# Groups of ten pairs in place of groups of four, six and eight, and another way for the down results, in a transformer block on one core

## The chip, the cores and the metric

One core of one Trainium2 chip runs the whole block. The metric is the device time of one execution in microseconds (us).

## The reference

The input is x, 2048 rows of 512, in f32. A vector c, through silu and a matrix, gives six modulation vectors (sa, ca, ga, sb, cb, gb). The block is

```python
h = _layernorm(x, axis=-1) * (1 + ca) + sa
x = x + ga * _A_ref(h, A_wqkv, A_wo)
h = _layernorm(x, axis=-1) * (1 + cb) + sb
x = x + gb * _B_ref(h, B_w_gate, B_w_up, B_w_down)
```

`_A_ref` is softmax attention with 32 heads of 16 columns over all 2048 rows, with an output projection wo. `_B_ref` is (silu(h @ w_gate) * (h @ w_up)) @ w_down with 1792 inner columns. All is f32, and the kernel keeps the accuracy by splitting operands into a high and a low part and adding three products.

## The kernel before

**Stages.** A projection stage (about the first tenth) makes q, k and v. Then comes attention, with the output projection and the feed-forward part of earlier rows woven into it, and at the end a tail with what is left of the third chunk and all of the fourth.

**Attention.** The 2048 query rows are four chunks of 512 (`NC`). A unit is one chunk with a group of four heads: `NU` = 32 units, eight to a chunk. A unit has 16 steps, one to each 128 keys, and a step has four pairs (`pair_of`). A pair is two matmuls of 512 columns that use different halves of TensorE's rows and run side by side: a score (line 507) and a maximum (line 478). The score goes through ScalarE's exp (line 509) into a tile `pt_` in SBUF. The maximum belongs to a unit 22 steps ahead: VectorE reduces its bank to one number for each row (line 480), which that unit's exps subtract later. For the last 22 steps no maximum is left. The product of exps and v comes later, by halves: a pv half (`pv_step`, line 522) is four heads by 256 columns, each in two passes, accumulated in bank 7. A step gives two halves. After a unit's last half ScalarE copies bank 7 to `o` (line 526), and the next unit's first half needs the bank empty.

**Order.** The order is written out by hand, as the Python code records it, and each engine works through its own list in that order. `plain(steps)` records windows of three pairs (`WIN`), after each of which some pv halves stand (`HALVES`). `filled(places, work)` records one group: after pair r it takes `places[r]` fills from `work`. A fill is two matmuls over 64 rows each (line 730), for two output banks side by side; the banks are 3 and 6 (`FBANKS`). Then it runs the callbacks in `posts` (`hook`) and those in `tails` (`flush`), and ends with pv halves (`pvs`). In a group the scores and maxima take five banks in turn (`five`: 0, 1, 2, 4, 5), a score and then its pair's maximum; behind the last maximum `ALONE` gives other places and banks for scores alone.

**What is woven in.** For each of the first three chunks: two output-projection tiles (`out_pair`, 24 fills each), a plain stretch of `NORM` and `WIN` steps for the layer norm, then the jobs of the feed-forward part: 14 gate/up tiles of 24 fills (`gate_up`) and 14 down tiles of 12 (`down`). The third chunk keeps its last seven jobs (`KEEP`) for the tail. The function `window` chooses the places. Early jobs are thin: `SIX`, six pairs and six fills to a group, four groups to a gate/up tile and two to a down tile. Later ones, from `THICK`, are thick: `TWO`, eight pairs and 12 fills, two groups to a gate/up tile, and `FOUR`, four pairs and six fills, two to a down tile. Projection tiles use `TWO`. The first down tile of the last pair of inner tiles has the places `LATE` where it is thin.

**Results of the tiles.** When a gate/up tile's fills end, ScalarE makes a tanh (`th`, line 783); at the group's end VectorE makes `q` and `m32` (lines 787 and 789) and GpSimd splits that into `mid`. When a down tile's fills end, VectorE adds both banks to the chunk's rows `x2` (line 803), at once, ahead of the reduces of the pairs that still follow in the group. After a chunk's last down tiles GpSimd's queue stores the rows (line 805) and loads those of the next chunk into the same `x2` (`rows_of`, line 642).

**Exp tiles.** `PTS` = 13 tiles `pt_` go round as a ring; a step's four tiles come free after its second pv half.

Of the kernel before, what the change touches and what calls it, by code (L numbers as in the profile page):

```python
# [9 lines left out]
F32 = mybir.dt.float32  # L10
# [9 lines left out]
P = 128  # L20
# [8 lines left out]
CW = S // NC  # L29
NG = H // 4  # L30
NU = NG * NC
NF = F // P
FG = 2
# [6 lines left out]
WIN = 3  # L40
HALVES = (2, 1, 1, 2)
ORDER = (0, 2, 1, 3)
UG = 16 * NG
PTS = 13
FBANKS = (3, 6)
KEEP = 7
NORM = 9
STARTS = (144, 272, 400)
REST = 12
THICK = (8, 8, 5)  # L50
TWO = (0, 3, 2, 2, 2, 2, 1, 0)
SIX = (0, 2, 2, 1, 1, 0)
FOUR = (0, 3, 3, 0)
LATE = (0, 0, 0, 3, 3, 0)
LAST = ((0, 4, 0, 4, 0, 4, 0, 0), (4, 5, 0, 1, 5, 0, 4, 1))
ALONE = {TWO: LAST, FOUR: ((0, 6, 0, 0), (4, 5, 0, 5)), SIX: ((0, 3, 0, 3, 0, 0), (4, 5, 0, 1, 4, 5))}


def run(it):
# [4 lines left out]
def take(it, k):  # L64
    run(islice(it, k))
# [40 lines left out]
def block_kernel(ctx, tc, x, wqkv, wo, w_gate, w_up, w_down, c, w_mod, out):  # L106
    nc = tc.nc
# [18 lines left out]
    four, bank, single = Turn(0, 1, 2, 3), Turn(4, 5, 6), Turn(7)  # L126
# [326 lines left out]
    pb = ctx.enter_context(tc.tile_pool(name="pb", bufs=2, reuse_waits="tile"))  # L453
    kop[1] = [pb.tile([P, 2, CW], F32R, name=f"kop1{c}", bufs=1) for c in range(NC)]
    pf = None
# [3 lines left out]
    qop, mx, pts, pv, o_, due, res = {}, {}, {}, {}, {}, {}, {}  # L459
    posts, tails = [], []  # L460
    n = 16 * NU
# [39 lines left out]
    def score(i, h):  # L501
        u, kt = divmod(i, 16)
        rows = slice(64 * (h % 2), 64 * (h % 2) + KR + 2)
        p_ = pb.tile([P, CW], F32, name="pt_", tag="pt", bufs=PTS)
        pts.setdefault(i, {})[h] = p_
        sp = bank("st_")
        nc.tensor.matmul(sp, kop[u % 2][kt // 4][rows, h // 2, kt % 4 * P:(kt % 4 + 1) * P], qop[u][rows, h // 2, :],  # L507
                         start=True, stop=True)
        nc.scalar.activation(p_, sp, AF.Exp, scale=SCALE)

    def pv_step(i, half):

        u, kt = divmod(i, 16)
        g = u % NG
        cols = slice(half * HQ, (half + 1) * HQ)
        if kt == 0 and half == 0:
            pv[u] = single("pv")
            o_[u] = pf.tile([P, CW], F32, name="o", tag="o", bufs=2)
        p_ = pts.pop(i) if half else pts[i]
        for h in range(4):  # L520
            e0 = (kt * H + 4 * g + h) * (DH + 1)
            nc.tensor.matmul(pv[u][32 * h:32 * h + 32, cols], v_flat[:, e0:e0 + 32], p_[h][:, cols],  # L522
                             start=(kt == 0 and half == 0), stop=(kt == 15),
                             skip_group_check=half == 1)
        if kt == 15 and half:
            nc.scalar.copy(o_[u], pv[u])  # L526
# [194 lines left out]
    def accumulate(outs, lhs, rhs, nk, after, halves, by_k=False):  # L721

        terms = [(k, a, b) for k in range(nk) for a, b in ((0, 0), (0, 1), (1, 0))]
        z = len(terms) - 1
        if halves:
            for ph in range(2):
                for j, (k, a, b) in enumerate(terms):
                    for e in range(2):
                        rows = slice(64 * (ph ^ e), 64 * (ph ^ e) + 64)
                        nc.tensor.matmul(outs[e], lhs(e, a, k)[rows], rhs(b, k)[rows],  # L730
                                         start=(ph == 0 and j == 0), stop=(ph == 1 and j == z))
                    if ph == 1 and j == z:
                        after()
                    yield
        else:
            order = [(e, j) for e in range(2) for j in range(z + 1)]
            for e, j in sorted(order, key=lambda o: o[1] // 3) if by_k else order:
                k, a, b = terms[j]
                nc.tensor.matmul(outs[e], lhs(e, a, k), rhs(b, k), start=(j == 0), stop=(j == z))  # L739
                if e == 1 and j == z:  # L740
                    after()
                yield
# [56 lines left out]
    def down(ch, m, t0, outs, halves):  # L799
        def later():  # L800
            for e in range(2):
                t = t0 + e
                nc.vector.tensor_add(ch.x2[:, t, :], outs[e], ch.x2[:, t, :])  # L803
                if m == NF // FG - 1:
                    (nc.sync if ch.ci == last else nc.gpsimd).dma_start(od[:, 4 * ch.ci + t, :], ch.x2[:, t, :])

        def after():
            if halves:
                later()
            else:  # L810
                posts.append(later)
            if t0:
                ch.load_wd(m + 1)

        mids, wd = [ch.mid[FG * m + k] for k in range(FG)], ch.wd[m]
        return accumulate(outs, lambda e, a, k: mids[k][:, a, (t0 + e) * P:(t0 + e + 1) * P],
                          lambda b, k: wd[:, b, k, :], FG, after, halves, m == NF // FG - 1)
# [20 lines left out]
    def hook():  # L838
        while posts:
            posts.pop(0)()  # L840

    def flush():
        while tails:
            tails.pop(0)()
# [66 lines left out]
    halves = [(i, half) for i in range(n) for half in range(2)]  # L911
    done, ended, owed = 0, 0, 0
# [13 lines left out]
    def pvs(most, by_halves):  # L926

        nonlocal owed
        if by_halves:
            most, owed = most + owed, 0  # L930
        while most and halves and 4 * halves[0][0] + (6 if done % 4 == 2 and not by_halves else 8) <= done:
            i, half = halves.pop(0)
            pv_step(i, half)
            most -= 1
            if i % 16 == 15 and half:
                close_unit(i // 16, done // 4 - 1)
                if by_halves:
                    break
        if by_halves and most and halves and 4 * halves[0][0] + 8 <= done:
            owed = most  # L940

    def end_steps():
        nonlocal ended
        while ended < done // 4:
            after(ended - 1)
            ended += 1

    def plain(steps, ends=()):

        nonlocal four, bank  # L950
        assert steps % WIN == 0 and done % 4 == 0
        four, bank = Turn(0, 1, 2, 3), Turn(4, 5, 6)
        for w in range(4 * steps // WIN):
            for _ in range(WIN):
                pair_of()
            if w >= 4 * steps // WIN - len(ends):
                ends[w - 4 * steps // WIN](four())
            flush()
            pvs((HALVES[(w - 2) % 4] if done > 8 else 0) + (w == 4 * steps // WIN - 1), True)
            end_steps()  # L960

    def filled(places, work):

        nonlocal four, bank
        four = bank = five
        if done >= 4 * n - 4 * (LEAD - 1):
            places, order = ALONE.get(places, (places, (4, 5, 0, 1)))
            bank = Turn(*order)
        for r in range(len(places)):
            pair_of()  # L970
            take(work, places[r])
            end_steps()
        hook()
        flush()
        pvs(3 if done % 4 else 6, False)

    def window(ch, job, args):
        thick = (args[0] if job is gate_up else 2 * args[0]) >= THICK[ch.ci]
        if job is down:
            if args == (NF // FG - 1, 0):  # L980
                return (FOUR, FOUR) if thick else (LATE, SIX)
            return (FOUR if thick else SIX,) * 2
        return (TWO,) * 2 if thick else (SIX,) * 4

    for k in range(NK):
        at(16 * (NU - 2) + 4 * k + 3, lambda k=k: chunks[last].load_wo_part(k))
    outs = [banks[b] for b in FBANKS]
    for ci in range(last):
        plain(STARTS[ci] - done // 4)
        ch = chunks[ci]  # L990
        for t0 in (0, 2):
            work = out_pair(ch, t0, outs, True)
            filled(TWO, work)
            filled(TWO, work)
        side.append(lambda: scaled(ch))
        plain(NORM)
        plain(WIN, [lambda tp, k=k: ch.turned(tp, k) for k in range(NK)])
        if ci == last - 1:
            plain(REST)
        for _ in range(len(ch.jobs) - (KEEP if ci == last - 1 else 0)):  # L1000
            job, args = ch.jobs.pop(0)
            if args == (NF // FG - 1, 0):
                chunks[ci + 1].load_wo()
            places = window(ch, job, args)
            work = job(ch, *args, outs, True)
            for group in places:
                filled(group, work)
        if ci < last - 1:
            rows_of(chunks[ci + 1])
    chunks[last - 1].load_gu(NF - 2)  # L1010

    assert done == 4 * n
    turns = chain([2, 3, 2, 0, 1, 2, 0], cycle([1, 3, 2, 0]))

# [11 lines left out]
    ch, chp = chunks[last], chunks[last - 1]  # L1026
# [56 lines left out]
```

## Time and profile before

| what | us |
|---|---|
| median of 3 runs (lowest to highest) | 1939.23 (1938.14 to 1940.55) |
| the profiled execution, its own time | 1938.7 |
| its span, first to last instruction | 1936.7 |
| TensorE busy | 1886.4 |
| VectorE busy | 1533.1 |
| ScalarE busy | 1235.0 |
| GpSimd busy | 386.5 |
| mean granted TensorE clock | 0.996 of full speed |

In the profile's rows PE is TensorE, DVE is VectorE, ACT is ScalarE and POOL is GpSimd. A row of the timeline has the start and the length in us, the engine, the line of the kernel, the operation, what it writes and reads, and how often; in brackets how long the engine was idle before it, and what ended that. In a grouped row the figures behind the bar are the busy time in us and the mean length of one in ns, and behind the next bar the idle time ahead of them. Matmuls overlap, and their ends are modelled, so their starts are what to read.

### The profile page before, as it was taken

To read this page: it belongs to the slowest core of one execution; us is meant where nothing else is said; L and a number is where in the kernel's file an instruction comes from. 1 tells how busy PE (TensorE), PEld (TensorE's weight loads), DVE (VectorE), ACT (ScalarE), POOL (GpSimd) and SP (SyncE) were. 2 spreads that over 40 slices of the span, in tenths; PEclk is the share of its full clock that TensorE was granted. 3 is DMA by queue.
4 is the path that set the end of the run, shared out by engine and by line. 5 is a ranking of instruction groups with operands and counts; after the bars stand their busy time and mean duration, and the time that the engine had idled before them with its cause. 6 is when DMAs were issued, how large, how long until landed. Compare 5 with 4: busy or idle time off the path is not lost.

```text
span 1936.7 us, 42054 instructions
## 1 busy us (share of the span) xinstructions
PE 1886.4 (97%) x16932; PEld 1231.0 (64%) x16932; DVE 1533.1 (79%) x2561; ACT 1235.0 (64%) x2330; POOL 386.5 (20%) x447
## 2 busy tenths in 40 slices
PE   7999999999999999999999999999999999997999
PEld 5766444444465666677765666677764666765887
DVE  5459999999988888888888888888889888811643
ACT  4221888888868666666667666666668666672211
POOL 3000544564213101011122101011122101120200
PEclk9999999999999999999999999999999999999999
DMA  8763655666424233334334233333433333334553
GB/s 285 276 216 120 202 174 170 199 188 202 138 75 124 75 105 124 97 116 131 110 112 136 69 110 116 113 118 111 128 106 108 92 98 116 108 134 147 180 189 109
DMA packets 102330, 267.63 MB, mean 138 GB/s; under 512 B 20552, under 2 KB 25672, under 8 KB 88952
## 3 DMA queue, kind: packets, MB, share of 16 engines
q1 hardware_dynamic: 86984, 202.27, 32.9%
q0 software_dynamic: 14464, 61.88, 9.0%
q8 instruction: 133, 2.18, 0.5%
q10 hardware_dynamic: 688, 0.80, 0.1%
q14 instruction: 61, 0.50, 0.1%
HBM read 201.85 MB, written 62.13 MB: 136 GB/s over the span
## 4 chain that ended last, share of the span: by engine, by line
PE 87%; DVE 7%; DMA 3%; ACT 2%; POOL 1%; issue 1%; SPq 0%; ACTq 0%; DVEq 0%; POOLq 0%
PE bank L522 23%; PE bank L507 19%; PE bank L730 18%; PE bank L478 11%; PE bank L739 7%; PE bank L213 7%; DVE mx L480 6%; DMA rb<-d_dr 1%; PE bank L491 1%; ACT o L526 1%; DMA dn<-o 0%; DMA d_dr<-dn 0%; PE bank L166 0%; PE bank L715 0%; DMA wm_ab<-in_w_mod 0%
## 5 line engine op out<-in xcount | busy, mean ns | idle before, releaser
L480 DVE TENSOR_REDUCE mx<-bank 128x1 f32<-128x512 f32 x2048 | 1277.9, 685 | 173.1 <-PE bank L478 133.5
L478 PE MATMUL bank<-kop,qop 48*128 48x512 f32 x2048 | 777.3, 445 | 2.3 <-DMA qop<-qd 1.5
L507 PE MATMUL bank<-qop,kop 50*128 50x512 f32 x2048 | 745.1, 422 | 3.3 <-DVE mx L480 1.2
L507 PEld LDWEIGHTS bank<-qop,kop 50*128 50x128 f32 x2048 | 347.1, 185 | 247.0 <-issue 44.1
L478 PEld LDWEIGHTS bank<-kop,qop 48*128 48x128 f32 x2048 | 343.5, 184 | 68.9 <-DVE mx L480 14.4
L730 PE MATMUL bank<-act,wgu 64*128 64x512 f32 x1872 | 356.1, 396 | 0.7 <-DVE m L789 0.6
L730 PEld LDWEIGHTS bank<-act,wgu 64*128 64x128 f32 x1872 | 236.5, 186 | 24.9 <-DVE m L789 4.2
L730 PE MATMUL bank<-wd,mid 64*128 64x512 f32 x912 | 168.8, 397 | 0.5 <-DVE m L789 0.4
L791 POOL CAST mid<-m 128x512 fp32r<-128x512 f32 x40 | 24.3, 608 | 537.3 <-DVE m L789 483.3
L730 PEld LDWEIGHTS bank<-wd,mid 64*128 64x128 f32 x912 | 112.8, 186 | 14.3 <-DVE m L789 3.2
L549 POOL TENSOR_TENSOR on<-o,rb 128x512 f32<-128x512 f32 x31 | 39.7, 1281 | 370.4 <-DMA rb<-d_dr 307.3
L213 PE MATMUL bank<-hT,wqs 128*128 128x512 f32 x384 | 96.1, 400 | 2.0 <-DVE prt L373 0.8
L787 DVE SCALAR_TENSOR_TENSOR q<-th,bank 128x512 f32<-128x512 f32 x56 | 38.0, 678 | 65.2 <-ACT th L783 65.2
L213 PEld LDWEIGHTS bank<-hT,wqs 128*128 128x128 f32 x384 | 70.2, 188 | 24.3 <-issue 6.0
L783 ACT ACTIVATE th<-bank 128x512 f32<-128x512 f32 x56 | 33.2, 594 | 58.8 <-PE bank L739 58.8
L803 DVE TENSOR_TENSOR x<-bank,x 128x512 f32<-128x512 f32 x84 | 53.7, 683 | 20.4 <-PE bank L507 20.4
L373 DVE TENSOR_TENSOR prt<-bank,prt 128x512 fp32r<-128x512 f32 x32 | 22.0, 689 | 46.7 <-ACT prt L371 44.6
L739 PE MATMUL bank<-act,kop 128*128 128x512 f32 x240 | 57.2, 396 | 0.0
L371 ACT CAST prt<-bank 128x512 fp32r<-128x512 f32 x32 | 18.8, 586 | 59.0 <-PE bank L213 50.6
L789 DVE TENSOR_TENSOR m<-bank,q 128x512 f32<-128x512 f32 x56 | 38.7, 692 | 22.0 <-PE bank L739 19.9
L739 PE MATMUL bank<-wd,mid 128*128 128x512 f32 x216 | 52.2, 395 | 0.3 <-DVE mid L792 0.3
L792 POOL TENSOR_TENSOR mid<-m,mid 128x512 fp32r<-128x512 f32 x40 | 51.5, 1288 | 3.3
(6272 smaller groups left out, 5132.9 us busy)
## 6 DMA issues: line engine op xcount, KB each, us to landing
kop<-kd SPq DMA_DIRECT2D x256, 192.0 KB
wgu<-gu_dr SPq DMA_DIRECT2D x46, 1024.0 KB
wd<-wd_dr SPq DMA_DIRECT2D x28, 1024.0 KB
gu_dr<-wgu POOLq DMA_DIRECT2D x14, 1024.0 KB, 6.7
qop<-qd SPq DMA_DIRECT2D x64, 192.0 KB
kop<-gu_dr SPq DMA_DIRECT2D x20, 512.0 KB
kd<-prt SPq DMA_DIRECT2D x16, 512.0 KB
qd<-prt SPq DMA_DIRECT2D x16, 512.0 KB
```

What stands on the lines that cost most here:

```text
L213: nc.tensor.matmul(pt, lhs(a, k), rhs(b, k), start=(n == 0), stop=(n == 3 * nk - 1))
L478: nc.tensor.matmul(pm, qop[u][rows, s, qt * P:(qt + 1) * P], kop[u % 2][kc][rows, s, :], start=True, stop=True)
L480: nc.vector.tensor_reduce(mx[u][:, b, s, qt, kc:kc + 1], pm, op=ALU.max, axis=AX.X)
L507: nc.tensor.matmul(sp, kop[u % 2][kt // 4][rows, h // 2, kt % 4 * P:(kt % 4 + 1) * P], qop[u][rows, h // 2, :], start=True, stop=True)
L522: nc.tensor.matmul(pv[u][32 * h:32 * h + 32, cols], v_flat[:, e0:e0 + 32], p_[h][:, cols], start=(kt == 0 and half == 0), stop=(kt == 15), ...
L549: mul.tensor_mul(on, o, rb)
L730: nc.tensor.matmul(outs[e], lhs(e, a, k)[rows], rhs(b, k)[rows], start=(ph == 0 and j == 0), stop=(ph == 1 and j == z))
L739: nc.tensor.matmul(outs[e], lhs(e, a, k), rhs(b, k), start=(j == 0), stop=(j == z))
L787: nc.vector.scalar_tensor_tensor(q, th, 1.0, outs[0], op0=ALU.add, op1=ALU.mult)
L789: nc.vector.tensor_mul(m32, outs[1], q)
L792: (nc.gpsimd if slow else nc.vector).tensor_sub(mid[:, 1, :], m32, mid[:, 0, :].bitcast(F32))
L803: nc.vector.tensor_add(ch.x2[:, t, :], outs[e], ch.x2[:, t, :])
```

## The change

- Groups: one shape, `TEN` (ten pairs, 12 fills), serves projection and gate/up tiles, two groups each; `FIVE` (five pairs, six fills) serves down tiles, two groups each; `LATE` is now a shape of five pairs. `window`, `THICK`, `TWO`, `SIX` and `FOUR` go. A chunk's woven work now takes 127 steps of 128, and the step left over is a plain stretch of its own.
- pv: a group ends with all halves of steps whose last score lies two pairs or more back, up to eight: six and four in turn after groups of ten; two, four, two, two after groups of five. A plain stretch ends with such a run as well, and may have a last window of fewer than three pairs. `REST` is 9 steps, not 12.
- Exp tiles: the ring is 15 long; 13 tiles lie where they lay, two (`FAR`) in the pool `pf`.
- Down results: in the groups ScalarE copies each bank to a temporary `part` and GpSimd adds that to `x2`. Both are recorded at the group's end. In the tail VectorE adds as before.

```diff
-PTS = 13
+PTS = 15
+FAR = 2
...
-REST = 12
-THICK = (8, 8, 5)
-TWO = (0, 3, 2, 2, 2, 2, 1, 0)
-SIX = (0, 2, 2, 1, 1, 0)
-FOUR = (0, 3, 3, 0)
-LATE = (0, 0, 0, 3, 3, 0)
...
+REST = 9
+TEN = (0, 2, 1, 2, 1, 2, 1, 3, 0, 0)
+FIVE = (0, 3, 1, 2, 0)
+LATE = (0, 0, 3, 3, 0)
+ALONE = {TEN: ((0, 4, 0, 4, 0, 4, 0, 0, 0, 0), (4, 5, 0, 1, 4, 5, 0, 1, 4, 5)),
+         FIVE: ((0, 3, 0, 3, 0), (4, 5, 0, 1, 5))}
...
-        p_ = pb.tile([P, CW], F32, name="pt_", tag="pt", bufs=PTS)
+        near = (4 * i + len(pts.get(i, ()))) % PTS < PTS - FAR
+        p_ = (pb if near else pf).tile([P, CW], F32, name="pt_", tag="pt", bufs=PTS - FAR if near else FAR)
...
-                nc.vector.tensor_add(ch.x2[:, t, :], outs[e], ch.x2[:, t, :])
+                if halves:
+                    part = pf.tile([P, CW], F32, name="part", tag="tmp", bufs=4)
+                    nc.scalar.copy(part, outs[e])
+                    nc.gpsimd.tensor_add(ch.x2[:, t, :], part, ch.x2[:, t, :])
+                else:
+                    nc.vector.tensor_add(ch.x2[:, t, :], outs[e], ch.x2[:, t, :])
...
-            if halves:
-                later()
-            else:
-                posts.append(later)
+            posts.append(later)
...
-        while most and halves and 4 * halves[0][0] + (6 if done % 4 == 2 and not by_halves else 8) <= done:
+        while most and halves and 4 * halves[0][0] + (8 if by_halves else 6) <= done:
...
-        pvs(3 if done % 4 else 6, False)
+        pvs(8, False)
...
-            places = window(ch, job, args)
             work = job(ch, *args, outs, True)
-            for group in places:
-                filled(group, work)
+            for i in range(2):
+                filled(TEN if job is gate_up else LATE if i == 0 and args == (NF // FG - 1, 0) else FIVE, work)
...
+    plain(n - done // 4)
```

On TensorE, the opening of a group of six of the first chunk's gate/up tiles before. Bank_63 to bank_70 are banks 0 to 7; `act` is the normed input (its two numbers are the high and the low part), `wgu` the weights, `qop` and `kop` are q and k.

```order
L507 MATMUL bank_64<-qop,kop_88 128x512
L478 MATMUL bank_65<-kop_972,qop 128x512
L507 MATMUL bank_67<-qop,kop_88 128x512
L478 MATMUL bank_68<-kop_972,qop 128x512
L730 MATMUL bank_66<-act_2642,wgu 128x512
L730 MATMUL bank_69<-act_2642,wgu 128x512
L730 MATMUL bank_66<-act_2643,wgu 128x512
L730 MATMUL bank_69<-act_2643,wgu 128x512
L507 MATMUL bank_63<-qop,kop_88 128x512
L478 MATMUL bank_64<-kop_973,qop 128x512
```

The opening of a group of ten at the same place of the program after the change:

```order
L507 MATMUL bank_63<-qop,kop_88 128x512
L477 MATMUL bank_64<-kop_973,qop 128x512
L507 MATMUL bank_65<-qop,kop_88 128x512
L477 MATMUL bank_67<-kop_973,qop 128x512
L730 MATMUL bank_66<-act_2642,wgu 128x512
L730 MATMUL bank_69<-act_2642,wgu 128x512
L730 MATMUL bank_66<-act_2643,wgu 128x512
L730 MATMUL bank_69<-act_2643,wgu 128x512
L507 MATMUL bank_68<-qop,kop_88 128x512
L477 MATMUL bank_63<-kop_973,qop 128x512
```

Up to the third pair nothing moved: two pairs, two fills, a pair, and in both the third pair's maximum takes the bank of the group's first score (bank_64 above, bank_63 here). What differs comes behind it: one fill instead of two before the fourth pair, and ten pairs instead of six before the pv halves.

On ScalarE, the end of the first down tile of the first chunk before: the exps (`pt`) of the last three pairs of its second group, then of the next group's first two.

```order
L509 ACTIVATE pt__7542<-bank_65 128x512
L509 ACTIVATE pt__7549<-bank_68 128x512
L509 ACTIVATE pt__7558<-bank_64 128x512
L509 ACTIVATE pt__7577<-bank_67 128x512
L509 ACTIVATE pt__7582<-bank_63 128x512
```

The end of the same down tile on ScalarE after the change, again the last three pairs' exps and the next two:

```order
L509 ACTIVATE pt__7494<-bank_63 128x512
L509 ACTIVATE pt__7501<-bank_65 128x512
L509 ACTIVATE pt__7510<-bank_68 128x512
L805 COPY part<-bank_66 128x512
L805 COPY part<-bank_69 128x512
L509 ACTIVATE pt__7537<-bank_64 128x512
L509 ACTIVATE pt__7542<-bank_67 128x512
```

The two reads of the down tile's banks stood on VectorE, ahead of the reduce of that group's last pair; now they stand on ScalarE, behind the group's last exp and ahead of the next group's first. VectorE has only reduces at that place. The additions stand on GpSimd, four in a row for the two down tiles that follow each other, behind the `mid` of the gate/up tile before them and ahead of the next unit's `on` (line 549) and the next tile's `mid`.

More of the change, by code (lines that the diff above doesn't have):

```diff
@@ L48 @@
 STARTS = (144, 272, 400)
-REST = 12
-THICK = (8, 8, 5)
-TWO = (0, 3, 2, 2, 2, 2, 1, 0)
-SIX = (0, 2, 2, 1, 1, 0)
-FOUR = (0, 3, 3, 0)
-LATE = (0, 0, 0, 3, 3, 0)
-LAST = ((0, 4, 0, 4, 0, 4, 0, 0), (4, 5, 0, 1, 5, 0, 4, 1))
-ALONE = {TWO: LAST, FOUR: ((0, 6, 0, 0), (4, 5, 0, 5)), SIX: ((0, 3, 0, 3, 0, 0), (4, 5, 0, 1, 4, 5))}
+REST = 9
[4 more added lines that the diff above has]
+         FIVE: ((0, 3, 0, 3, 0), (4, 5, 0, 1, 5))}
 def run(it):
@@ L950, in plain @@
         nonlocal four, bank
-        assert steps % WIN == 0 and done % 4 == 0
+        assert done % 4 == 0
         four, bank = Turn(0, 1, 2, 3), Turn(4, 5, 6)
-        for w in range(4 * steps // WIN):
-            for _ in range(WIN):
+        groups = [WIN] * (4 * steps // WIN) + [4 * steps % WIN] * (4 * steps % WIN > 0)
+        for w, pairs in enumerate(groups):
+            for _ in range(pairs):
                 pair_of()
-            if w >= 4 * steps // WIN - len(ends):
-                ends[w - 4 * steps // WIN](four())
+            if w >= len(groups) - len(ends):
+                ends[w - len(groups)](four())
             flush()
-            pvs((HALVES[(w - 2) % 4] if done > 8 else 0) + (w == 4 * steps // WIN - 1), True)
+            pvs((HALVES[(w - 2) % 4] if done > 8 else 0) + (w == len(groups) - 1), True)
             end_steps()
+        pvs(8, False)
     def filled(places, work):
@@ L974, in filled @@
         flush()
-        pvs(3 if done % 4 else 6, False)
[L977 to L983, printed above, removed]
+        pvs(8, False)
     for k in range(NK):
@@ L992, in block_kernel @@
             work = out_pair(ch, t0, outs, True)
-            filled(TWO, work)
-            filled(TWO, work)
+            filled(TEN, work)
+            filled(TEN, work)
         side.append(lambda: scaled(ch))
```

## The prediction

> **What bounds the kernel now.** I read the page first, then TensorE's rows in the timeline through one group of each kind, then ScalarE's, VectorE's and GpSimd's rows beside them.
>
> ```profile
> PE 1886.4 (97%) x16932; PEld 1231.0 (64%) x16932; DVE 1533.1 (79%) x2561; ACT 1235.0 (64%) x2330; POOL 386.5 (20%) x447
> ...
> PEclk9999999999999999999999999999999999999999
> ...
> PE 87%; DVE 7%; DMA 3%; ACT 2%; POOL 1%; issue 1%; SPq 0%; ACTq 0%; DVEq 0%; POOLq 0%
> ...
> L480 DVE TENSOR_REDUCE mx<-bank 128x1 f32<-128x512 f32 x2048 | 1277.9, 685 | 173.1 <-PE bank L478 133.5
> ```
>
> TensorE holds 87% of the chain that ended last, at full granted clock, so the question is what the change saves on TensorE. The 97% hides how dense its work is. That is read in the timeline, below through the last group of eight pairs of a gate/up tile (from 880.85) and the first group of four pairs of a down tile (from 887.72); the columns are start, length, instruction.
>
> ```profile
> 880.85 0.49 PE L507 MATMUL bank<-qop,kop 50*128 50x512 f32 x1
> ...
> 881.42 0.86 PE L730 MATMUL bank<-act,wgu 64*128 64x512 f32 x6
> 882.11 0.40 PE L507 MATMUL bank<-qop,kop 50*128 50x512 f32 x1
> ...
> 885.40 0.40 PE L507 MATMUL bank<-qop,kop 50*128 50x512 f32 x1
> ...
> 887.72 0.49 PE L507 MATMUL bank<-qop,kop 50*128 50x512 f32 x1
> ...
> 891.32 0.50 PE L507 MATMUL bank<-qop,kop 50*128 50x512 f32 x1
> ```
>
> A pair (score and maximum side by side) or a fill (two 64-row products side by side) takes one slot. From the third pair (882.11) to the eighth (885.40) lie 14 slots, 3.29 us, so a slot is 0.235 us. The group of eight lasts 6.87 us, the group of four 3.60 us, and inside neither does TensorE pause: both are nothing but slots, pv halves and two switches.
>
> The group of six pairs does pause:
>
> ```profile
> 775.21 0.50 PE L507 MATMUL bank<-qop,kop 50*128 50x512 f32 x1
> ...
> 775.77 0.63 PE L730 MATMUL bank<-act,wgu 64*128 64x512 f32 x4
> 776.25 0.39 PE L507 MATMUL bank<-qop,kop 50*128 50x512 f32 x1
> 776.45 0.49 PE L478 MATMUL bank<-kop,qop 48*128 48x512 f32 x1
> ...
> 777.01 0.39 PE L507 MATMUL bank<-qop,kop 50*128 50x512 f32 x1
> ...
> 778.19 0.39 PE L507 MATMUL bank<-qop,kop 50*128 50x512 f32 x1
> 778.56 0.40 PE L522 MATMUL bank<-pt__8724,v_flat 128*32 128x256 f32 x1
> ...
> 779.66 0.38 PE L522 MATMUL bank<-pt__8766,v_flat 128*32 128x256 f32 x1
> ...
> 779.99 0.50 PE L507 MATMUL bank<-qop,kop 50*128 50x512 f32 x1
> ```
>
> The third pair's score starts at 776.25, its maximum 0.20 us later. With five banks in turn that maximum takes the bank of the first score, and must wait until ScalarE has read it:
>
> ```profile
> 775.80 0.60 ACT L509 ACTIVATE pt__8766<-bank 128x512 f32<-128x512 f32 x1 [1.35 <-PE bank L478]
> 776.29 0.59 ACT L509 ACTIVATE pt__8771<-bank 128x512 f32<-128x512 f32 x1
> 776.77 0.61 ACT L509 ACTIVATE pt__8780<-bank 128x512 f32<-128x512 f32 x1
> 777.48 0.60 ACT L509 ACTIVATE pt__8789<-bank 128x512 f32<-128x512 f32 x1
> ```
>
> The first exp ends at 776.40, the maximum starts at 776.45. In the group of eight three fills, not two, stand ahead of the third pair, and nothing is late. A pv half is two passes; six passes start between 778.56 and 779.66, 0.22 apart, so a half is 0.44. This group lasts 4.78, the next one 4.86 (it ends at 784.85); I use 4.82.
>
> ```profile
> 784.85 0.50 PE L507 MATMUL bank<-qop,kop 50*128 50x512 f32 x1
> ```
>
> **Filled groups, with maxima.** By the code's thresholds there are 128 groups of six before, 41 of eight and 24 of four (7 of eight and 8 of four more come after the last maximum): 128 x 4.82 + 41 x 6.87 + 24 x 3.60 = 617.0 + 281.7 + 86.4 = 985.1 us for 1192 pairs. After it there are 86 groups of ten and 68 of five, 1200 pairs, the eight more being taken from plain windows.
>
> A group of ten opens like one of six (pair, pair, two fills, pair), so I let it pay the same pause. Walked on, a pair's maximum needs the exp two pairs back: 0.47 to 0.52 after that score starts (777.01 to 777.48, 776.25 to 776.77), 0.60 long, 0.05 to tell, 1.12 to 1.17 together. Places 1, 2, 1, 2, 1 put five slots, 1.175, between such pairs, so no second pause follows. The reduces keep ahead too:
>
> ```profile
> 775.77 3.80 DVE L480 TENSOR_REDUCE mx<-bank 128x1 f32<-128x512 f32 x6 [0.88 <-PE bank L478]
> ```
>
> A score needs the bank of the maximum three pairs back. The first reduce starts 0.56 into the group, six take 3.80, the last of them 0.69, so they start 0.62 apart; the seventh ends near 0.56 + 6 x 0.62 + 0.69 = 4.97, and the tenth pair, which needs it, starts near 5.3. A group of ten is then the group of six with ten slots and two halves more: 4.82 + 2.35 + 0.88 = 8.05; walked place by place, 5.34 for the last pair, 0.37 to the first pv, 5 x 0.44, 0.12 back, it is 8.03. I take 8.03. Low end: the group of eight with two slots and a half more and no pause, 6.87 + 0.47 + 0.44 = 7.78. High end: what 10 pairs and 12 fills cost today on average of thin and thick, (4 x 4.82 + 2 x 6.87) / 4 = 8.26.
>
> A group of five has three fills ahead of its third pair, like the group of four, hence no pause: 3.60 + one slot + half a pv half = 4.06. High end, the same average: 4.21.
>
> 86 x 8.03 + 68 x 4.06 = 690.6 + 276.1 = 966.7 against 985.1: **-18.4 us**.
>
> **Behind the last maximum.** Two scores share a slot there.
>
> ```profile
> 1705.83 0.50 PE L507 MATMUL bank<-qop,kop 50*128 50x512 f32 x2
> ...
> 1711.69 0.50 PE L507 MATMUL bank<-qop,kop 50*128 50x512 f32 x2
> ...
> 1724.49 0.66 PE L507 MATMUL bank<-qop,kop 50*128 50x512 f32 x2
> ```
>
> One group of eight takes 5.86, four of four 12.80, so 3.20 each: 7 x 5.86 + 8 x 3.20 = 66.6. After: 4 groups of ten at 5.86 + 0.235 + 0.44 = 6.54, 8 of five at 3.20 + 0.235 + 0.22 = 3.66, four scores alone for about 2.5: 57.9. **-8.7 us**: more fills have gone where maxima run beside them.
>
> **The o copy.** Where a pv stretch holds the end of one unit and the start of the next, TensorE waits for bank 7 to be copied:
>
> ```profile
> 649.86 0.38 PE L522 MATMUL bank<-pt__7175,v_flat 128*32 128x256 f32 x1
> ...
> 650.96 0.40 PE L522 MATMUL bank<-pt__7226,v_flat 128*32 128x256 f32 x1 [0.70 <-ACT o L526]
> ```
>
> 1.10 where a pass takes 0.22: 0.88 lost. By the order this falls inside a stretch 16 times before and 11 times after: **-4.4 us**.
>
> **Plain windows.** There VectorE sets the pace:
>
> ```profile
> 263.82 21.88 DVE mx L480 x37
> ```
>
> 21.88 / 37 = 0.59 a pair. Four pairs fewer are 2.4 saved; two stretches of a single step between chunks, worth 2.36 at that pace, cost about 2.65 (the fourth score waits for the first exp until 1.24, 0.4 to the pv, two halves, 0.12 back): +0.6. **-1.8 us**.
>
> **Down results.** 76 additions leave VectorE; 76 copies go to ScalarE and 76 additions to GpSimd.
>
> ```profile
> 888.28 1.91 DVE L480 TENSOR_REDUCE mx<-bank 128x1 f32<-128x512 f32 x3
> ...
> 891.89 1.91 DVE L480 TENSOR_REDUCE mx<-bank 128x1 f32<-128x512 f32 x3 [0.77 <-PE bank L507]
> 893.72 1.29 DVE L803 TENSOR_TENSOR x<-bank,x 128x512 f32<-128x512 f32 x2
> ```
>
> Removing them gains TensorE nothing by itself: VectorE idles 0.77 us in that group with them. The copies stand behind the group's last exp, and behind them stand the next group's exps. The last pair of five starts at 2.45, its exp at 2.95; the copies follow 0.49 apart, as exps do, and end at 4.52. Banks 3 and 6 are wanted by the next fill at 4.06 + 0.57 = 4.63, and the first exp could start at 4.65. Only where two pv halves stand between (the second half of a tile) is the group 3.84 long, and both are some 0.1 to 0.15 late, 19 times. **+3 us**, from 0 to the price in the third rival. GpSimd's additions hold nobody until the ring of four temporaries comes round, more than 15 us later. At a chunk's end they delay the stores and the x load queued behind them:
>
> ```profile
> 977.70 0.78 POOL L642 DMA_DIRECT2D x<-in_A_x  x1 [2.64 <-DMA out<-x]
> ```
> ```profile
> DMA to landing us min/median/max: 5.5/6.3/9.6
> ```
>
> With two copies and two additions of 1.3 they come some 3.5 us later, but the load's reader also comes later, by 2.65 + 2 x (8.03 - 6.87) = 5.0. Nothing.
>
> Fifteen exp tiles are what ten pairs need: at most five are held when a group opens. So the ring costs nothing; with 13 the last pairs would wait for pv.
>
> **Sum.** -18.4 - 8.7 - 4.4 - 1.8 + 3 = -30.3. The profiled execution took 1938.7 (span 1936.7 and 2.0 around it), 0.5 under the median of 1939.2: 1938.7 - 30.3 = 1908.4, **1908 us**.
>
> **Rivals.** (1) No pause in the group of ten: 86 x 0.25 = 21.5 less, 1887. For it: the group of eight runs so. Against it: two fills, not three, ahead of the third pair, as in the group of six. (2) A pair and its fills cost what they cost today on average, because another wait takes the pause's place: 86 x 8.26 + 68 x 4.21 = 996.7, 30.0 more, 1938, no change. Against it: walked through, both kinds have a bank free in time; for it: the margin over the exp two pairs back is 0.05 or less. (3) Slower: ScalarE becomes what the pairs wait for. In a down tile the copies delay the next group's exps one for one, each at its full 0.60, and the maxima two pairs on with them: 38 tiles x 1.20 = 45.6 instead of 3, 1951. It outweighs the rest from 0.88 us a tile. Against it: ScalarE is idle 36% of the span, mostly in pv stretches, where the copies lie. (4) GpSimd's additions hold VectorE off: 76 x 1.29 = 98 us, of which the groups of five, with five reduces 0.6 apart each, can hide 68 x (4.06 - 3.00) = 72: 26 more, 1934. Against it:
>
> ```profile
> 888.97 1.29 POOL L792 TENSOR_TENSOR mid<-m,mid 128x512 fp32r<-128x512 f32 x1
> ```
>
> Beside this two-operand GpSimd operation three reduces took 1.91, as the three from 891.89 did without one. [...] That the code does not do what it says is no rival: the order shows the groups, the copies and the additions.
>
> **Chances.** Forecast 0.64, (1) 0.17, (2) 0.08, (3) 0.07, (4) 0.04. A measurement of this kernel tells about 0.2% (4 us) from no change. Faster: forecast, (1) and (4), 0.85; same: (2), 0.08; slower: (3), 0.07. The range takes in the forecast with a group of ten between 7.9 and 8.2 and up to 10 us of new waits (1897 to 1928) and (1) with no copy wait and a little over (1882); the other three, 0.19, lie outside: 1882 to 1928.
>
> **What would show it.** In the changed kernel's timeline: groups of ten about 8.03 from first pair to first pair with one gap of 0.2 ahead of the third maximum; groups of five 4.06; 11 waits for the o copy; copies that end before the next group's first exp. A group of ten at 7.8 makes (1) right, at 8.26 with gaps elsewhere (2); exps that start late behind copies in every group after a down tile make (3) right, and a reduce that lasts over 0.7 beside a GpSimd addition (4). I am wrong altogether if neither kind of group is cheaper per pair than the average of today (8.26 and 4.21).

## The result and the profile after

| | before | after |
|---|---|---|
| median of 4 runs (lowest to highest), us | 1938.97 (1938.14 to 1940.55) | 1905.13 (1903.83 to 1909.28) |
| profiled execution, its own time, us | 1938.7 | 1905.84 |
| its span, us | 1936.7 | 1904.0 |

The ratio is 0.9828, with a 95% interval of 0.9811 to 0.9845: 33.8 us faster. 1908 was forecast, and the forecast's case is the one that came.

The page of the changed kernel, the lines that answer to those shown of before:

```profile
PE 1859.4 (98%) x16932; PEld 1212.7 (64%) x16932; DVE 1470.5 (77%) x2485; ACT 1251.3 (66%) x2406; POOL 483.5 (25%) x523
...
PE 91%; DVE 3%; DMA 2%; ACT 2%; issue 0%; SPq 0%; POOL 0%; ACTq 0%; DVEq 0%; POOLq 0%
...
L479 DVE TENSOR_REDUCE mx<-bank 128x1 f32<-128x512 f32 x2048 | 1259.7, 684 | 203.4 <-PE bank L477 149.9
...
L806 POOL TENSOR_TENSOR x<-part,x 128x512 f32<-128x512 f32 x76 | 96.4, 1289 | 203.5 <-ACT part L805 203.4
```

TensorE has the same 16932 matmuls, and its share of the chain that ended last grew from 87% to 91%, while VectorE's fell from 7% to 3%. VectorE has 76 instructions fewer, ScalarE and GpSimd 76 more each: the additions have moved.

Where did the time come from? The first and the last start of three kinds of instruction cut the span into stages: the first fill that reads `wgu` first, the last reduce, the last copy to `o`. Before:

```profile
L730 PE MATMUL bank<-wgu,act x288: 385/393/495, 543.5 to 1432.4; 64*128 64x512 f32 x144
```
```profile
L480 DVE TENSOR_REDUCE mx<-bank x2048: 627/682/699, 130.6 to 1690.9; 128x1 f32<-128x512 f32 x187
```
```profile
L526 ACT COPY o<-bank x32: 585/586/617, 234.0 to 1762.0; 128x512 f32<-128x512 f32 x32
```

After:

```profile
L730 PE MATMUL bank<-wgu,act x288: 383/393/499, 542.4 to 1414.4; 64*128 64x512 f32 x144
```
```profile
L479 DVE TENSOR_REDUCE mx<-bank x2048: 627/682/698, 129.3 to 1665.7; 128x1 f32<-128x512 f32 x187
```
```profile
L526 ACT COPY o<-bank x32: 586/588/619, 232.7 to 1730.4; 128x512 f32<-128x512 f32 x32
```

| stage | before | after | difference |
|---|---|---|---|
| up to the first fill | 543.5 | 542.4 | -1.1 |
| first fill to last reduce | 1147.4 | 1123.3 | -24.1 |
| last reduce to last copy to `o` | 71.1 | 64.7 | -6.4 |
| from there to the end of the span | 174.7 | 173.6 | -1.1 |

The two middle stages, which hold the changed groups, give -30.5. The outer two, -2.2 together, do the same arithmetic in both kernels; I do not put them down to the change, though the way of the down results reaches into the tail, as the part on the prediction shows.

Now the groups. TensorE through a group of ten with six pv halves (from 744.47) and into the next, with four (from 752.90):

```profile
744.47 0.50 PE L507 MATMUL bank<-qop,kop 50*128 50x512 f32 x1
...
745.50 0.40 PE L507 MATMUL bank<-qop,kop 50*128 50x512 f32 x1
745.66 0.50 PE L477 MATMUL bank<-kop,qop 48*128 48x512 f32 x1
...
749.86 0.39 PE L507 MATMUL bank<-qop,kop 50*128 50x512 f32 x1
750.17 0.40 PE L522 MATMUL bank<-pt__8430,v_flat 128*32 128x256 f32 x1
...
752.90 0.49 PE L507 MATMUL bank<-qop,kop 50*128 50x512 f32 x1
...
760.54 0.50 PE L507 MATMUL bank<-qop,kop 50*128 50x512 f32 x1
```

The first exp of that group on ScalarE:

```profile
745.01 0.60 ACT L509 ACTIVATE pt__8493<-bank 128x512 f32<-128x512 f32 x1 [1.39 <-PE bank L507]
```

It ends at 745.61 and the third pair's maximum starts at 745.66, 0.16 behind its score: the forecast gap, for the forecast reason. The last pair comes 5.39 into the group (5.34 forecast). The two groups last 8.43 and 7.64, 8.04 in the mean; 8.03 was forecast.

Four groups of five in a row, two down tiles, on TensorE:

```profile
764.63 0.50 PE L507 MATMUL bank<-qop,kop 50*128 50x512 f32 x1
...
769.34 0.49 PE L507 MATMUL bank<-qop,kop 50*128 50x512 f32 x1
...
773.17 0.50 PE L507 MATMUL bank<-qop,kop 50*128 50x512 f32 x1
...
777.03 0.49 PE L507 MATMUL bank<-qop,kop 50*128 50x512 f32 x1
```

With the start at 760.54 above they last 4.09, 4.71 (four halves), 3.83 and 3.86: 4.12 in the mean, 4.06 forecast.

The two copies of the last of these groups, on ScalarE:

```profile
776.68 1.07 ACT L805 COPY part<-bank 128x512 f32<-128x512 f32 x2
```

They end at 777.75, 0.72 into the next group, where the fills stand 0.57 in: the second of the two banks is late. The first line below says how long TensorE's weight loads (PEld) for the fills waited for the copies in the whole trace after the change (us, times). The other two say what TensorE waited for at `o` (us, times, longest), before and after:

```profile
  PEld bank L730: 4.2, 17
```
```profile
PE bank L522 <- ACT o L526: 12.5, 16, 1.1
```
```profile
PE bank L522 <- ACT o L526: 8.3, 11, 1.1
```

17 waits for copies, 19 forecast; 11 waits at `o`, 4.2 us fewer than with 16.

### The profile page after: what moved, and what is told of

It reads as the page before. It is cut to its first block, busy times and chain, and to the rows that moved or that the text cites. A ratio compares the mean times of both kernels' runs of the same rounds, so it can differ in the third digit from the quotient of the medians.

```text
span 1904.0 us, 42175 instructions
## 1 busy us (share of the span) xinstructions
PE 1859.4 (98%) x16932; PEld 1212.7 (64%) x16932; DVE 1470.5 (77%) x2485; ACT 1251.3 (66%) x2406; POOL 483.5 (25%) x523
## 4 chain that ended last, share of the span: by engine, by line
PE 91%; DVE 3%; DMA 2%; ACT 2%; issue 0%; SPq 0%; POOL 0%; ACTq 0%; DVEq 0%; POOLq 0%
PE bank L522 25%; PE bank L507 20%; PE bank L730 19%; PE bank L477 12%; PE bank L739 7%; PE bank L212 7%; DVE mx L479 2%; PE bank L490 1%; DMA dn<-o 1%; DMA kop<-kd 0%; PE bank L165 0%; ACT o L526 0%; PE bank L715 0%; DVE stt L755 0%; DMA wm_ab<-in_w_mod 0%
## 5 line engine op out<-in xcount | busy, mean ns | idle before, releaser
L479 DVE TENSOR_REDUCE mx<-bank 128x1 f32<-128x512 f32 x2048 | 1259.7, 684 | 203.4 <-PE bank L477 149.9
L730 PEld LDWEIGHTS bank<-act,wgu 64*128 64x128 f32 x1872 | 229.1, 186 | 21.0 <-ACT part L805 4.2
L730 PE MATMUL bank<-wd,mid 64*128 64x512 f32 x912 | 151.2, 394 | 0.1
L806 POOL TENSOR_TENSOR x<-part,x 128x512 f32<-128x512 f32 x76 | 96.4, 1289 | 203.5 <-ACT part L805 203.4
L730 PEld LDWEIGHTS bank<-wd,mid 64*128 64x128 f32 x912 | 97.4, 186 | 13.4 <-DVE m L789 1.8
L783 ACT ACTIVATE th<-bank 128x512 f32<-128x512 f32 x56 | 33.5, 598 | 71.1 <-PE bank L739 59.1
L730 PE MATMUL bank<-wgu,act 64*128 64x512 f32 x288 | 55.4, 398 | 0.1
```

What stands on the lines that cost most here:

```text
L479: nc.vector.tensor_reduce(mx[u][:, b, s, qt, kc:kc + 1], pm, op=ALU.max, axis=AX.X)
L783: nc.scalar.activation(th, outs[0], AF.Tanh, scale=0.5)
L806: nc.gpsimd.tensor_add(ch.x2[:, t, :], part, ch.x2[:, t, :])
```

## The experiments

My theory was that of the prediction: a group costs its slots, its halves and its switch, and on top a pause wherever a maximum reaches its bank before the exp that empties it; fewer, longer groups pay fewer switches and fewer pauses, and the route of the down results gives nothing. Rivals: the length of the groups alone decides and the pause costs nothing in the end; or the gain comes from freeing VectorE of the additions.

**Does the third fill ahead of the third pair save the pause?** Groups of ten opened like the group of eight:

```diff
-TEN = (0, 2, 1, 2, 1, 2, 1, 3, 0, 0)
+TEN = (0, 3, 1, 2, 1, 2, 1, 2, 0, 0)
```

> The changed kernel (1905.1) with three fills instead of two ahead of the third pair of a group of ten, and two instead of three ahead of the last two pairs. Pause theory (a maximum must wait for the exp two pairs back, so two pairs need five slots between them; a group of ten with 12 fills cannot avoid one such pause, and it costs about 0.29 us at the opening, where the two halves of TensorE's rows also fall out of step, and about 0.18 at the end, where pv follows anyway): 0.1 us less in each of 86 groups, 1896 (1890 to 1901). Length theory (the gain comes from fewer and longer groups alone, each group less saving one switch to pv and back, 0.41): the same 12 fills and ten pairs, no difference, 1905.

Measured: 1904.73, ratio 0.9823 (0.981 to 0.9837), the same as the change. The sum of the pause theory failed here, and the trace shows where; TensorE at the same place:

```profile
744.34 0.50 PE L507 MATMUL bank<-qop,kop 50*128 50x512 f32 x1
...
745.61 0.42 PE L477 MATMUL bank<-kop,qop 48*128 48x512 f32 x1
745.62 0.39 PE L507 MATMUL bank<-qop,kop 50*128 50x512 f32 x1
...
749.25 0.62 PE L507 MATMUL bank<-qop,kop 50*128 50x512 f32 x2
749.67 0.49 PE L477 MATMUL bank<-kop,qop 48*128 48x512 f32 x1
750.09 0.40 PE L522 MATMUL bank<-pt__8432,v_flat 128*32 128x256 f32 x1
...
752.82 0.50 PE L507 MATMUL bank<-qop,kop 50*128 50x512 f32 x1
```

The gap at the opening is gone: the third pair starts side by side at 745.61. But the fill that went to the front is missing near the end, where the ninth and tenth scores start one behind the other (749.25, two in a row) and the last maximum follows them at 749.67. The pv halves come only at 750.09, and the group lasts 8.48. Over the whole trace the groups of ten with four halves have the median of the change, 7.63, and those with six halves a higher one, 8.79 against 8.58. Twelve fills do not cover both ends of ten pairs.

**The same fill taken away from the group of five:**

```diff
-FIVE = (0, 3, 1, 2, 0)
+FIVE = (0, 2, 2, 2, 0)
```

> The changed kernel with two fills instead of three ahead of the third pair of a group of five (places 0, 2, 2, 2, 0). Pause theory: the third maximum waits 0.2 us for the first exp and another 0.05 to 0.1 is lost in getting in step again, in each of 68 groups with maxima: 17 to 20 us more, 1922 to 1925. Length theory: as many pairs, fills and switches, 1905.

Measured: 1914.17, ratio 0.9874 (0.9861 to 0.9888), 9 us above the change. The last two groups of the place shown above:

```profile
769.09 0.50 PE L507 MATMUL bank<-qop,kop 50*128 50x512 f32 x1
...
773.11 0.50 PE L507 MATMUL bank<-qop,kop 50*128 50x512 f32 x1
...
777.18 0.50 PE L507 MATMUL bank<-qop,kop 50*128 50x512 f32 x1
```

4.02 and 4.07 stand here for 3.83 and 3.86 there: the pause is real, but it costs 0.2 a group, not the 0.25 to 0.3 that I had put into the expectation; over 68 groups the 9 us are 0.13 each. The theory that length alone decides falls.

**The down results back on VectorE, the groups as changed:** the additions stand where they stood before, ahead of the last reduces.

```diff
-                if halves:
+                if False:
...
-            posts.append(later)
+            if halves:
+                later()
+            else:
+                posts.append(later)
```

> The changed kernel with the down results added by VectorE at once, as before the change, in place of ScalarE's copies and GpSimd's additions; groups, exp tiles and pv as changed. Pause theory: VectorE has about 1 us to spare in a group of five, and the copies cost 3 us or less, so 1902 to 1908. Route theory (a good part of the 34 us comes from VectorE's being freed of 76 additions, 52 us): 10 us or more is lost, 1915 or above.

Measured: 1901.63, ratio 0.981 (0.9796 to 0.9823). By the medians the groups alone are worth all of the gain and about 3.5 us more. The intervals of this kernel and of the change overlap, so by itself this is a hint; the pair `nine` and `nine_vector` below says it again.

**The route alone, the groups as before:** of the change's diff only the two pieces of `down`, the copy with the addition and `posts.append(later)`.

> The kernel before, its groups of four, six and eight and its 13 exp tiles, with only the down results changed: copied by ScalarE and added by GpSimd at the group's end. Pause theory: VectorE had time for the additions and the copies cost up to 0.15 us a tile, so 0 to 6 us more than before, 1939 to 1945. Route theory: freeing VectorE of 52 us shortens the groups of six, 1933 or less.

Measured: 1947.61, ratio 1.0041 (1.0028 to 1.0053): 8 us slower, and above the 1939 to 1945 expected by the pause theory. The theory that the route brings the gain falls. Part of the loss has a place. Behind a chunk's end the projection tile waits for the rows that GpSimd's queue loads; the group on TensorE, and VectorE's first instruction in it:

```profile
989.10 0.49 PE L507 MATMUL bank<-qop,kop 50*128 50x512 f32 x1
...
990.29 1.33 PE L730 MATMUL bank<-wgu,act 64*128 64x512 f32 x5 [0.46 <-DVE x L751]
...
997.80 0.50 PE L507 MATMUL bank<-qop,kop 50*128 50x512 f32 x1
```
```profile
989.54 1.29 DVE L751 TENSOR_TENSOR x<-bank,x 128x512 f32<-128x512 f32 x2 [1.45 <-DMA x<-in_A_x]
```

The same group before:

```profile
988.82 0.49 PE L507 MATMUL bank<-qop,kop 50*128 50x512 f32 x1
...
996.44 0.50 PE L507 MATMUL bank<-qop,kop 50*128 50x512 f32 x1
```

8.70 instead of 7.62, and at the next chunk 8.81 instead of 7.63: 2 us. In the changed kernel TensorE has no such wait there. By the stages of the table above, this execution lost 3.9 us between the first fill and the last reduce, these 2 among them, 2.2 from there to the last copy to `o`, and 2.6 in the tail.

**Only groups of five, four to a gate/up or projection tile:** here the projection tiles, and the loop of jobs likewise.

```diff
-            filled(TEN, work)
-            filled(TEN, work)
+            for _ in range(4):
+                filled(FIVE, work)
```

> The changed kernel with groups of five in place of every group of ten: four of them to a gate/up or projection tile. Pause theory: two groups of five cost 8.12 to 8.19 against 8.05 for one of ten, because what a second switch costs (0.41) is nearly paid by the pause that a group of five does not have (0.29): 0.07 to 0.14 us in each of 86 groups with maxima, and 3 us behind the last maximum, 1914 (1910 to 1920). Length theory: each of 86 more groups costs a switch of 0.41, 35 us, all of the gain: 1940.

Measured: 1933.76, ratio 0.9974 (0.9964 to 0.9983). Neither theory had this. The trace shows the cover that was lost. VectorE's `m` where a gate/up tile ends:

```profile
647.49 0.69 DVE L789 TENSOR_TENSOR m<-bank,q 128x512 f32<-128x512 f32 x1
```

And TensorE's next group:

```profile
647.05 0.50 PE L507 MATMUL bank<-qop,kop 50*128 50x512 f32 x1
...
648.24 0.96 PE L730 MATMUL bank<-act,wgu 64*128 64x512 f32 x5 [0.23 <-DVE m L789]
...
651.61 0.50 PE L507 MATMUL bank<-qop,kop 50*128 50x512 f32 x1
```

`m` is what empties the second bank of the fills, and it ends at 648.18, 1.13 into a group whose fills stand 0.57 in. That group lasts 4.56 with two halves; in the changed kernel such groups lasted 3.83 and 3.86. Behind a group of ten the same thing is small: the group of five from 760.54 above, the first behind a gate/up tile, took 4.09. In this trace `m` ends within the first 2 us of 30 groups of five with two halves; beyond 3.86 each they take 26 us together, most of the 28.6 that this kernel loses against the change. A group of five with two halves has no room for `q` and `m` beside its five reduces: in this trace the five before them take 3.11 us, `q` 0.68 and `m` 0.69, together 4.48 on VectorE, more than the 3.83 to 3.86 of such a group in the changed kernel.

**Two fives and a ten to such a tile,** so that `q` and `m` follow a long group:

```diff
-            filled(TEN, work)
-            filled(TEN, work)
+            for group in (FIVE, FIVE, TEN):
+                filled(group, work)
```

> The changed kernel with two groups of five and one of ten, in this order, for each gate/up and projection tile. It asks why four groups of five took 1933.8 and not 1914. Late-result theory: a group of five in the middle of a tile costs 4.08, and what was dear is the end of a gate/up tile, where VectorE makes q and m only after the group's reduces, and two halves of pv (0.9 us) are too short to hide that; a group of ten at the end hides it. Then two of five and one of ten are 16.21 against 16.10: 43 x 0.11 + 2 = 7 more than 1905, 1912 (1907 to 1917). If groups of five are dear wherever they stand (1020.5 us for 240 of them, 4.25), they are 16.55: 43 x 0.45 + 2 = 21 more, 1926.

Measured: 1906.28, ratio 0.9832 (0.9813 to 0.9852). It is some 6 us better than I expected; 5 waits at `o` in place of 11, 3.6 us in place of 8.3, are most of that. Without the waits at `o` its groups with maxima take 995.4 us against 989.8 in the change: 5.6 more. For these 43 tiles the late-result theory had 4.7 more, and the theory that fives are dear in themselves 19. So with the late result out of the way two fives cost little more than a ten.

**A group in which both ends are covered:** nine pairs with 12 fills, in 80 of the 86 groups (the last gate/up tiles of the third chunk keep `TEN`); the pairs left over go to plain windows.

```diff
-REST = 9
+REST = 13
+NINE = (0, 3, 1, 2, 1, 2, 1, 2, 0)
```

> The changed kernel with groups of nine pairs and 12 fills (places 0, 3, 1, 2, 1, 2, 1, 2, 0) in place of 80 of its 86 groups of ten; the 80 pairs go to plain windows, at about 0.60 each, and REST is 13 steps. Nine pairs are the most that 12 fills can keep five slots apart two by two, so by the pause theory such a group has no pause at either end: 21 slots at 0.235, 4.5 halves at 0.44 and 0.41 for the switch are 7.33 against 8.05 measured for ten. 80 x 0.72 = 58 less, 80 x 0.60 = 48 more: 1895 (1888 to 1901). Length theory (a pair in a group costs its slot and its pv, 0.455, whatever the places): 80 x 0.455 = 36 less, 48 more: 1917.

Measured: 1900.32, ratio 0.9798 (0.9784 to 0.9811). TensorE at the starts of three such groups, the first two of them with four halves (the score is line 508 here):

```profile
717.93 0.50 PE L508 MATMUL bank<-qop,kop 50*128 50x512 f32 x1
...
725.09 0.50 PE L508 MATMUL bank<-qop,kop 50*128 50x512 f32 x1
...
732.24 0.50 PE L508 MATMUL bank<-qop,kop 50*128 50x512 f32 x1
```

They last 7.16 and 7.15, where a group of ten with four halves took 7.64. The halves are the same, one slot of the difference is the pair that is missing (0.235), and the other 0.25 is the pause that went. The pause theory holds against length, though only 5 of the 10 us came that I had expected below the change. Of the traces' own sums, the groups with maxima gained 55.0 us where 58 were expected, and the plain windows with the 80 pairs cost 48.1, as expected.

**The same with VectorE's additions,** by the edit of `down_by_vector`:

> The kernel with groups of nine, and the down results added by VectorE at once as before the change. If the copies cost what the kernel with VectorE's additions alone showed, 3.5 us, this is 3 to 4 us below the kernel with groups of nine: 1891 by the pause theory, 1913 by the length theory. If VectorE's additions and shorter groups get in each other's way, it is not below it.

Measured: 1896.03, ratio 0.9772 (0.9759 to 0.9786), 4.3 below `nine`, and the lowest run of `nine` (1899.62) is above the highest here (1897.1). The route costs about as much as the prediction said; where it costs that is another matter, as the part on the prediction shows.

**Where the units change.** The starts of the chunks' woven work moved by one step and by two, on the last kernel, so that by the order 3 and 9 stretches of pv halves cross from one unit to the next, in place of 12:

```diff
-STARTS = (144, 272, 400)
-REST = 13
+STARTS = (145, 273, 401)
+REST = 12
```

> The kernel with groups of nine and VectorE's additions (1896.0), every chunk's woven work begun one step later and REST one step shorter. Nothing changes but where a unit ends in its pv stretch: with the start of the next unit behind it in the same stretch, so that TensorE must wait for the copy of bank 7, in 3 places instead of 12. At 0.88 to 0.95 a place that is 8 less: 1888 (1884 to 1891). If the copy is hidden anyway or the wait only moves, 1896.

> The same with two steps, where 9 places are left: 3 less than 1896, 1893, and 5 more than with one step. If the later start itself is what helps, it is at least as fast as with one step.

Measured: 1884.18, ratio 0.9719 (0.9705 to 0.9733), and 1889.51, ratio 0.9748 (0.9735 to 0.9761). TensorE's waits at `o` with no shift, one and two:

```profile
PE bank L523 <- ACT o L527: 9.5, 13, 1.1
```
```profile
PE bank L523 <- ACT o L527: 2.5, 3, 1.1
```
```profile
PE bank L523 <- ACT o L527: 6.8, 9, 1.1
```

Between the two shifts lie 5.3 us, and 6 crossings of 0.88 are 5.3. Both came about 4 us lower than expected from `nine_vector`. The kernel before took 1938.33 beside these two and 1939.88 beside `nine_vector`, which may be 1.6 of it; the rest is open. One step later is the fastest kernel of this study, 2.8% below before; its interval lies clear of that of the change (0.9811 to 0.9845).

## Why the prediction was right

**The filled groups (-18.4 forecast).** I added up all groups with maxima, each from its first score to the next group's. Before, 193 groups took 1018.7 us, of which 12.5 are waits at `o`: 1006.2. After, 154 took 997.0, less 7.2 at `o` (the eleventh wait there lies behind the last maximum) and 3.7 for copies: 986.1. That is -20.1. The price of a clean group held: the medians are 4.85, 6.89 and 3.61 before (4.82, 6.87 and 3.60 in the sum), and 8.58 and 7.63 for groups of ten with six and four halves after, 8.10 in the mean (8.03). All groups at these medians would give 989.9 and 973.6, -16.3. But both totals are some 20 us above the sum, 1006.2 against 985.1 and 986.1 against 966.7, because I had priced clean groups only. This error stood on both sides and nearly cancelled, which was luck. One of the waits that I had not priced is TensorE's for `m` ahead of the fills (us, times), before and after:

```profile
  DVE m L789: 8.4, 22
```
```profile
  DVE m L789: 5.0, 23
```

It fell by 3.4, which is about as much as -20.1 lies beyond the -16.3 of the medians.

**Why longer groups are cheaper.** In the prediction's units the group of eight, 6.87, is 20 slots, four halves of 0.44 and 0.41 for the switch. Taken so, the slots of all groups with maxima cost 610.1 before and 620.4 after (more fills stand beside maxima), the halves 262.2 and 264.0, and the switches 193 x 0.41 = 79.1 and 154 x 0.41 = 63.1. What is left of 1018.7 and 997.0 I count as waits: 67.3 and 49.5. So the change lost 12 on slots and halves, and won 16 on switches and 18 on waits, the pauses, the o copies and `m` among them. `ten_three_first` and `nine` show that the pause belongs to ten pairs with twelve fills and not to the opening alone, which the prediction had not seen: it named the opening as the place, and with the opening cured the end paid the same.

**Behind the last maximum (-8.7).** The table's stage gives -6.4. The four whole groups of ten there had been priced at 6.54 and took 7.20 in the mean, with one wait at `o` of 1.1 us among them; the eight of five took 3.56 (3.66). The last maximum now falls inside a group of ten, so that part of a mixed group is counted there too. Both middle stages together were forecast at -30.3 and measured at -30.5.

**The plain windows (-1.8)** took 131.2 us before and 130.7 after, from the first fill on. `ten_three_first` and `five_two_first`, with the same windows as the change, took 127.5 and 127.9, so one execution does not settle so small a term.

**The o copy (-4.4)** measured -4.2. The waits in these traces are 0.73 to 0.83 each in the mean, and the two shifts lie 0.88 a crossing apart, the prediction's price.

**The down results (+3)** measured 3.5 and 4.3, but the place was not the one in the prediction, and that the number came out is luck. The waits for copies in the second half of a down tile are there. Yet the groups with maxima as a whole are hardly dearer with the copies than with VectorE's additions: 997.0 us against 997.5 in `down_by_vector`, and 941.9 in `nine` against 940.6 in `nine_vector`. With VectorE's additions TensorE's weight loads for the scores wait for those, 30 times and 12.4 us in `down_by_vector`; the sum had put them at nothing.

Most of what the profiled executions differ by lies behind the last reduce, to the end of the span: 238.3 us against 236.1, and 238.6 against 234.8. The six traces of the changed kernel and its variants with the copies have 237.1 to 240.0 there, the four with VectorE's additions 233.2 to 236.1. Two things differ there. The copies of the last woven down tile stand on the chain that ended last, for 0.98 us, just ahead of the last scores. And GpSimd's queue issues the load of the last chunk's rows behind its additions, 13.7 us later than without them, after the change and in `down_by_vector`:

```profile
1729.32 0.77 POOL L642 DMA_DIRECT2D v_flat<-in_A_x  x1
```
```profile
1715.58 0.78 POOL L642 DMA_DIRECT2D v_flat<-in_A_x  x1
```

So this load now leaves just ahead of the transfers that turn the last `o` into the operand of the tail, for which TensorE then stands still: 8.48 us against 7.54, and 8.21 in `nine` against 5.90 in `nine_vector`. In `route_only` the load leaves 19.5 us later than before, and TensorE stands still for 11.65 us against 9.99. That the load causes the longer stop is not shown, since no run moves the load alone, and the stops overlap: `ten_three_first`, with the copies, has one of 7.05.

**The x load ("nothing")** was right inside the woven part of the change, where TensorE's scores waited 0.5 us in all for the additions behind that load. For the last chunk's load it is in doubt, as just said. With the groups of before (`route_only`) there is no slack for it in the woven part either.

**The rivals.** (1), no pause, fell by the gap at 745.50 to 745.66. (2), the average conserved, fell by the medians. (3), ScalarE as the bound, fell by 4.2 us of waits in place of 45.6. (4), VectorE held off, fell by the reduces: with 76 GpSimd additions of 1289 ns their mean is 684 ns and the longest of the 2048 takes 698, against 685 and 699 before.

## What to carry to other kernels

When an engine is near 100% busy, price its work in the units in which it repeats, and look for what is neither unit: here the switch between kinds of tiles and a bank that is not yet read. Fewer and longer groups saved both here, 16 and 18 us by the count above, but only as long as the fills cover the first and the last pairs, and as long as another engine's results at the group's end (`m` here) still have their idle time. Before an addition is moved off an engine that waits anyway, ask what it would gain, and what stands behind it in the queue that it moves to: here it cost 3.5 and 4.3 us, and a late load stood behind it.

## What the runs showed of the hardware that was not expected

Five executions of `fives_then_ten` lasted from 1903.54 us, at a mean granted clock of 0.998, to 1913.08 at 0.993. The clocks stand in the ratio 1.005, and so do the times. So a few us between single profiled executions may be clock alone. In the changed kernel's trace the clock falls where TensorE stands still in the tail, from 1750.0 to 1758.45 (columns: window, length, busy time of PE, PEld, DVE, ACT and POOL with their instructions, granted clock, DMA share, GB/s):

```profile
1750.00:1755.00 5.00, 0.00 (x0) 0.00 (x0) 0.08 (x1) 0.00 (x0) 0.00 (x0) 0.73 0.20 73
1755.00:1760.00 5.00, 1.55 (x4) 1.23 (x5) 1.44 (x3) 1.12 (x2) 0.00 (x0) 0.50 0.18 51
```

In the first window no matmul runs, and in the second the granted clock is 0.50, when the work comes back. So here the fall goes with a gap of 8.48 us. But the clock also falls where no such gap stands. Twice in this trace, in the plain windows, it is 0.50 for 3.4 us, the second time from about 1008.2; the first time, and the 3.3 us ahead of it:

```profile
585.00:588.30 3.30, 2.98 (x20) 1.24 (x23) 3.23 (x9) 2.48 (x6) 1.71 (x9) 1.00 0.93 352
588.30:591.70 3.40, 3.40 (x26) 1.47 (x22) 2.73 (x5) 1.26 (x4) 2.88 (x9) 0.50 0.32 58
```

TensorE was busy for 2.98 of these 3.30 us. What sets the clock back there is open.
